# A Fourier transform and a soft mixture of experts on one core: z in token quarters with VectorE's block transposes, a in two row halves, groups of six slots, and a float32 output on 16 tiles

## The chip, the cores and the metric

The kernel runs on one core of one Trainium2 chip. The metric is device microseconds of one execution, the median over several runs. PE is TensorE (PEld its weight loads), DVE is VectorE, ACT is ScalarE, POOL is GpSimd, SP is SyncE, which issues the DMAs.

## The reference

Eight sequences of 2496 tokens with 256 values each go through a Fourier transform over the tokens and over the values, of which the real part is kept. The 19968 tokens then go through a soft mixture of eight experts with four slots each:

```
X = real(fft(fft(x, axis=1), axis=2))          # x: 8 x 2496 x 256
logits = X @ phi                               # X as 19968 x 256; 32 slots
d = exp(logits - logits.max(0)); d /= d.sum(0) + 1e-9      # over tokens
slot_input = (d.T @ X).reshape(8, 4, 256)
slot_out[e] = relu(slot_input[e] @ w1[e]) @ w2[e]          # 256 -> 1024 -> 256
c = exp(logits - logits.max(1)); c /= c.sum(1) + 1e-9      # over slots
out = c @ slot_out                             # 19968 x 256
```

All of it is in float32.

## The kernel before, in words

The transformed tokens are never formed. Since the logits are linear in x, phi is transformed first (psphi, wphi), x is multiplied with it, and the Fourier transform over the tokens is then made on 32 slot columns instead of 256 values. In the same way the weights d are transformed back and multiplied with x. The 2496 tokens are taken as 64 x 39, by a length-64 and a length-39 transform; symmetry folds 39 to 20. Two sequences are a pair (two times 64 rows), so there are four pairs, p = 0 to 3, each of five loads of x of about 1 MB into a ring of six tiles.

The program is a list of parts (ORDER), each a letter with one or two indices. A scheduler then sets the order on each engine from it.

- a(p, u) folds x on VectorE into eo (L222 to L227), transposes it on PE (pt, L231), which ScalarE copies to et (L232), and multiplies with the transformed phi on four column tiles of 32 (z, L238). ScalarE copies z to zs (L246).
- t(p) turns z back to token rows: ten PE transposes a pair (zt, L259), copied by ScalarE with a stride into the tile zt (L262, L266).
- b(p) is the length-64 transform: 11 groups of three slots of both sequences, one matmul over 128 rows each (a, L275), copied to o1 (L282).
- c(p, half) is the length-39 part: lp and lm (L293, L294), the logits lt (L295 to L298), the maxima over tokens (mx, mt, mall; L301 to L313), exp into d (L316, one a group) and its sum and difference dpm (L318, L319).
- e and d transform the weights back (e, L331, L340; d, L348) into ds (copies L356, some on VectorE); tok sums them; u multiplies with eo (L373).
- w loads w1 and w2 into the ring and the eo tiles, m merges the pairs, l and v are the experts' two layers (h, L472, with VectorE's block transpose L484; so, L492), and r replicates slot_out (sorep, L510).
- s(p) is the softmax over slots: PE turns the logits (cT, L529), ScalarE copies them to c (L534). In two halves follow the maximum (VectorE, L543), a subtraction (GpSimd, L544), exp (ScalarE, L545), the sum (VectorE, L546), 1e-9 and the reciprocal (L547, L548), and the product (GpSimd, L549).
- q(p, half) splits c into a high and a low part in a rounded float32 format, fp32r (hl, L555, L556); r did the same with slot_out (rh).
- o(p, b) is a megabyte of output: four PE transposes of hl (lT, L569), a ScalarE copy (L570), four times two matmuls of 128x512 (po, L576), eight evictions' worth of copies shared by ScalarE and VectorE (L580, 512 columns each) and the DMA (L587; the last rows of a pair go to out0, L585).

The PSUM banks of 512 columns are shared in small rings: two, three, two and one.

Of the kernel before, what the change touches and what calls it, by code (L numbers as in the profile page):

```python
# [7 lines left out]
F32R = mybir.dt.float32r  # L8
# [7 lines left out]
NPAIR = 4  # L16
D = 256
NSLOT = 32
GS = 3
NG = 11  # L20
GH = ((0, 6), (6, 5))
RING = 6
EOB = 3
CAFTER = 1
# [3 lines left out]
LT = 4  # L28
CT = ['sa', 'lt', 'lt', 'lt']
HT = ['se', 'zs']  # L30
RH = 0
LATE = 'zs'
SEB = 2
DE = 4
GP = 3
FIRST = [0, 1]
# [13 lines left out]
def _tables():  # L50
# [13 lines left out]
    eye = np.eye(2 * GS)  # L64
# [4 lines left out]
    def block(t):  # L69
# [15 lines left out]
        ("wa", np.block([[np.cos(al), np.sin(al)], [-np.sin(al), np.cos(al)]])),  # L85
# [15 lines left out]
        ("sel", np.arange(6)[:, None] + 6 * (np.arange(256) // 128) == np.tile(s, 2) // GS),  # L101
# [15 lines left out]
def _build(nc, tc, xh, phih, w1h, w2h, cins, where, out, out0):  # L117
# [4 lines left out]
    with ctx:  # L122
        cp = ctx.enter_context(tc.tile_pool(name="cp", bufs=1))
        sb = ctx.enter_context(tc.tile_pool(name="sb", bufs=1))
        pp = ctx.enter_context(tc.tile_pool(name="pp", bufs=P2, space=PSUM))
        p1 = ctx.enter_context(tc.tile_pool(name="p1", bufs=P1, space=PSUM))
        pu = ctx.enter_context(tc.tile_pool(name="pu", bufs=1, space=PSUM))
# [13 lines left out]
        def bufs_(tag):  # L141
            return {"zs": 2, "sa": 2, "se": SEB, "lt": LT}[tag]
# [7 lines left out]
        def bank1(name, dt=F32):  # L150
            return p1.tile([128, 512], dt, name=name, tag="p1")

# [45 lines left out]
        mall = cp.tile([6, 2, NPAIR, GS], F32, name="mall")  # L198
# [9 lines left out]
        zs, zt, o1, dpm, esb, dsb = {}, {}, {}, {}, {}, {}  # L208

        def part_a(p, u):  # L210
            qs = [2 * u, 2 * u + 1] if u < 2 else [4]
            nq = len(qs)
            if u == 0:
                eo[p] = [eu(f"eo{p}_{t}") for t in range(5)]
                zs[p] = sb.tile([128, 10, 128], F32, name=f"zs{p}", tag="zs", bufs=2)
            tr = []
            for k in range(2):
                tr.append(et([128, 4, 2, nq, NA], f"et{p}_{u}_{k}"))
            for qi, t in enumerate(qs):
# [8 lines left out]
                for k in range(2):  # L228
                    b = bank1(f"pt{p}_{t}_{k}")
                    for g in range(4):  # L230
                        pe.transpose(b[:, g * 128 : g * 128 + 128], e[:, g, k * 128 : k * 128 + 128], ident)  # L231
                    sc.copy(tr[k][:, :, :, qi, :], b.rearrange("p (g h a) -> p g h a", g=4, h=2))  # L232
            z = bank1(f"z{p}_{u}")
            n = 128 * nq
            for i, (w, k) in enumerate(((0, 0), (1, 1), (2, 1))):
                o = 0 if i < 2 else n
                for g in range(4):
                    pe.matmul(  # L238
                        z[32 * g : 32 * g + 32, o : o + n],
                        wphi[:, w, :],  # L240
                        tr[k][:, g].rearrange("p h q a -> p (h q a)"),
# [4 lines left out]
            sc.copy(  # L246
                zs[p][:, 4 * u * 1 : 4 * u + 2 * nq, :].rearrange("p i (r a) -> p r i a", r=2),
                z[:, : 2 * n].rearrange("p (r i a) -> p r i a", r=2, a=NA),
            )


        def part_t(p):
            zt[p] = sa([128, GS * NG, 2, NKC], f"zt{p}")
            nc.gpsimd.memset(zt[p][:, NSLOT:], 0.0)
            for b, units in enumerate(([(0, q) for q in range(4)], [(1, q) for q in range(4)], [(0, 4), (1, 4)])):
                ps = bank(f"zt{p}_{b}")
                for i, (h, q) in enumerate(units):
                    u, nq = q // 2, 2 if q < 4 else 1
                    pe.transpose(ps[:, i * 128 : i * 128 + 128], zs[p][:, 4 * u + nq * h + q % 2], ident)  # L259
                if b < 2:  # L260
                    dst = zt[p][:, :NSLOT, b, 0:16].rearrange("p s c -> p c s")
                    sc.copy(dst, ps.rearrange("p (c s) -> p c s", s=NSLOT))  # L262
                else:
                    for h in range(2):
                        dst = zt[p][:, :NSLOT, h, 16:20].rearrange("p s c -> p c s")
                        sc.copy(dst, ps[:, h * 128 : h * 128 + 128].rearrange("p (c s) -> p c s", s=NSLOT))  # L266

        def part_b(p):
            o1[p] = sa([120, 2, NG, NA], f"o1{p}")
            for b in range(3):  # L270
                ps = bank(f"a{p}_{b}")
                n = min(4, NG - 4 * b)
                for i in range(n):
                    g = 4 * b + i
                    pe.matmul(  # L275
                        ps[:120, i * 128 : i * 128 + 128],
                        zt[p][:, GS * g : GS * g + GS].rearrange("p s h c -> p (s h c)"),
                        C("wa"),
                        start=True,
                        stop=True,  # L280
                    )
                sc.copy(o1[p][:, :, 4 * b : 4 * b + n, :], ps[:120, : n * 128].rearrange("p (u r k) -> p r u k", u=n, r=2))  # L282

        def part_c(p, hf):
            g0, n = GH[hf]
            w = n * NA
            if hf == 0:
                lt[p] = sb.tile([120, NG, 2, NA], F32, name=f"lt{p}", tag="lt", bufs=LT)
            L = lt[p][:, g0 : g0 + n]
            pl = bank(f"lp{p}_{hf}")  # L290
            pm = bank(f"lm{p}_{hf}")
            mv = o1[p][:, :, g0 : g0 + n].rearrange("p r u k -> p r (u k)")
            pe.matmul(pl[:120, :w], C("wcc"), mv[:, 0], start=True, stop=True)  # L293
            pe.matmul(pm[:120, :w], C("wcs"), mv[:, 1], start=True, stop=True)  # L294
            sc.copy(L[:, :, 0], pl[:120, :w].rearrange("p (g n) -> p g n", g=n))  # L295
            pmv = pm[:120, :w].rearrange("p (g n) -> p g n", g=n)
# [3 lines left out]
            mx = sb.tile([120, 6], F32, name=f"mx{p}_{hf}", tag="mx", bufs=2)[:, :n]  # L300
            v.tensor_reduce(mx, L.rearrange("p g s n -> p g (s n)"), axis=AX.X, op=ALU.max)  # L301
            if PM:
                ps = pp.tile([128, 512], F32, name=f"mt{p}_{hf}", tag="pm", bufs=PM)
            else:
                ps = bank3(f"mt{p}_{hf}")
            pe.transpose(ps[:n, :120], mx, ident[:120, :120])
            m = mall[:n, hf, p]
            v.tensor_reduce(m, ps[:n, :120].rearrange("p (s k) -> p s k", s=GS), axis=AX.X, op=ALU.max)
            mex = sb.tile([6, GS, 40], F32, name=f"mex{p}_{hf}", tag="mex", bufs=1)[:n]
            v.tensor_scalar(mex, m.unsqueeze(2).to_broadcast([n, GS, 40]), -1.0, None, op0=ALU.mult)  # L310
            pe.transpose(ps[:120, 128 : 128 + n], mex.rearrange("p s k -> p (s k)"), ident[:n, :n])
# [3 lines left out]
            for g in range(n):  # L315
                sc.activation(d[:, g], L[:, g], AF.Exp, bias=nm[:, g : g + 1], scale=1.0)  # L316
# [341 lines left out]
```

## Time and profile before

| | us |
|---|---|
| median of 3 runs | 200.26 (199.95 to 200.35) |
| the profiled execution | 201.22 |
| its span in the profile | 199.4 |
| PE busy | 174.7 (88%) |
| VectorE, ScalarE busy | 131.8, 132.4 (66% each) |
| GpSimd busy | 24.6 (12%) |
| read from and written to HBM | 38.46 MB, 20.45 MB |

The span runs from the first to the last event that the profiler sees on the core; the profiled execution's own time holds 1.8 us more around it. The rows of the profile have the form "line engine operation out<-in shape xcount | busy, mean ns of one | idle time before, and what ended it". In a chain or a timeline a row is "start us, us, what". The mean granted clock of PE was 0.979 of full.

### The profile page before, as it was taken

The numbers are of one execution on the slowest core, as the hardware profiler recorded it, in microseconds if no ns is written. First come the engines' busy times: TensorE is split into PE (matmuls) and PEld (weight loads), VectorE is DVE, ScalarE is ACT, GpSimd is POOL, SyncE is SP. The second block draws the span as 40 slices with busy tenths as digits, with TensorE's granted clock in tenths as the row PEclk, the third lists the DMA queues.
The fourth block names the chain that finished last, engine by engine and source line by source line (L and its number), as shares of the span: only waits on it lengthen the run. The fifth ranks groups of instructions, "written<-read, shape, count | busy, mean of one in ns | idle before, by whom it ended". The sixth has DMA issues, their size and how long they took to land.

```text
span 199.4 us, 4290 instructions
## 1 busy us (share of the span) xinstructions
PE 174.7 (88%) x1690; PEld 125.6 (63%) x1690; DVE 131.8 (66%) x238; ACT 132.4 (66%) x277; POOL 24.6 (12%) x27
## 2 busy tenths in 40 slices
PE   0499889969999999989999989999999999989900
PEld 0375575549666877556865859346788877768700
DVE  0599856989993991742357624796677888976700
ACT  2135775579876795687856963763867988896610
POOL 0000000000000000000000100767101357320000
PEclk9999999997999999999999999999999999999995
DMA  5999999998880499600393687991099999799996
GB/s 183 409 427 410 422 420 420 419 391 291 301 363 21 112 358 424 263 0 0 111 283 138 205 326 234 364 404 58 2 378 355 419 409 389 306 421 363 430 426 214
DMA packets 10707, 59.17 MB, mean 297 GB/s; under 512 B 1344, under 2 KB 1728, under 8 KB 5696
## 3 DMA queue, kind: packets, MB, share of 16 engines
q1 hardware_dynamic: 10688, 58.91, 76.0%
q8 instruction: 13, 0.21, 0.4%
q14 instruction: 6, 0.05, 0.1%
HBM read 38.46 MB, written 20.45 MB: 295 GB/s over the span
## 4 chain that ended last, share of the span: by engine, by line
PE 75%; ACT 10%; DMA 2%; DVE 2%; issue 2%; POOL 2%; SPq 0%; ACTq 0%; DVEq 0%; POOLq 0%
PE po L576 17%; PE pt L231 9%; PE z L238 7%; PE a L275 6%; PE e L331 6%; PE u L373 5%; PE d L348 4%; PE h L472 4%; PE so L492 3%; PE lp L293 3%; PE lm L294 3%; PE cT L529 2%; DMA x<-xh 2%; ACT zt L262 2%; PE lT L569 2%
## 5 line engine op out<-in xcount | busy, mean ns | idle before, releaser
L576 PE MATMUL po<-rh,lTs 128*128 128x512 f32 x160 | 42.4, 405 | 1.5 <-ACT lTs L570 0.7
L231 PE MATMUL pt<-cs,eo 128*128 128x128 f32 x160 | 26.9, 300 | 8.9 <-DVE eo L226 7.9
L576 PEld LDWEIGHTS po<-rh,lTs 128*128 128x128 f32 x160 | 28.1, 188 | 8.5 <-ACT o L580 1.8
L232 ACT COPY et<-pt 128x512 f32<-128x512 f32 x40 | 23.1, 592 | 13.8 <-PE pt L231 13.2
L580 DVE COPY o<-po 128x512 f32<-128x512 f32 (+1 forms) x40 | 26.9, 686 | 7.9 <-PE po L576 7.0
L231 PEld LDWEIGHTS pt<-cs,eo 128*128 128x128 f32 x160 | 19.9, 153 | 15.9 <-DVE eo L226 7.9
L580 ACT COPY o<-po 128x512 f32<-128x512 f32 x40 | 23.2, 595 | 7.3 <-PE po L576 7.1
L224 DVE TENSOR_TENSOR x<-x 128x1024 f32<-128x1024 f32 x16 | 19.5, 1217 | 3.0 <-DMA x<-xh 3.0
L238 PE MATMUL z<-et,wphi 128*32 128x256 f32 (+1 forms) x288 | 19.0, 371 | 1.9 <-ACT et L232 1.8
L544 POOL TENSOR_TENSOR c<-c,cm 128x640 f32<-128x640 f32 x8 | 11.8, 1489 | 28.0 <-DVE cm L543 27.0
L316 ACT ACTIVATE d<-lt,nm 120x128 f32<-120x128 f32 x44 | 13.6, 390 | 1.9 <-DVE nm L313 1.8
L226 DVE TENSOR_TENSOR eo<-x 128x512 f32<-128x512 f32 x20 | 13.6, 682 | 0.6 <-PE u L373 0.3
L238 PEld LDWEIGHTS z<-et,wphi 128*32 128x32 f32 x288 | 7.8, 113 | 9.4 <-ACT et L232 4.2
L227 DVE TENSOR_TENSOR eo<-x 128x512 f32<-128x512 f32 x20 | 13.6, 680 | 0.0
L331 PE MATMUL e<-cs,dpm 120*64 120x120 f32 x176 | 13.5, 273 | 0.0
L331 PEld LDWEIGHTS e<-cs,dpm 120*64 120x64 f32 x176 | 10.7, 136 | 3.5 <-issue 2.4
L356 ACT COPY ds<-d 64x320 f32<-64x320 f32 x24 | 10.0, 421 | 4.2 <-PE d L348 3.5
L275 PE MATMUL a<-cs,zt 128*120 128x128 f32 x88 | 12.2, 292 | 0.4 <-ACT zt L266 0.3
L275 PEld LDWEIGHTS a<-cs,zt 128*120 128x120 f32 x88 | 11.1, 196 | 1.9 <-ACT zt L266 1.3
L549 POOL TENSOR_TENSOR c<-c,cm 128x640 f32<-128x640 f32 x8 | 11.0, 1391 | 10.0 <-DVE cm L548 5.5
L570 ACT CAST lTs<-lT 128x512 fp32r<-128x512 f32 x20 | 11.5, 599 | 0.9 <-PE lT L569 0.9
L373 PE MATMUL u<-eo,ds 128*32 128x129 f32 x320 | 11.6, 275 | 0.0
(99 smaller groups left out, 251.4 us busy)
## 6 DMA issues: line engine op xcount, KB each, us to landing
x<-xh SPq DMA_DIRECT2D x16, 1024.0 KB, 11.3
out<-o SPq DMA_DIRECT2D x15, 1024.0 KB, 5.6
w<-w1h SPq DMA_DIRECT2D x6, 1024.0 KB, 8.6
w<-w2h SPq DMA_DIRECT2D x12, 512.0 KB, 6.0
x<-xh SPq DMA_DIRECT2D x4, 896.0 KB, 10.3
out<-o SPq DMA_DIRECT2D x4, 768.0 KB, 6.0
w<-w1h SPq DMA_DIRECT2D x4, 512.0 KB, 5.2
w<-w2h SPq DMA_DIRECT2D x2, 1024.0 KB, 8.0
```

The costliest lines, as they stand in the source:

```text
L224: v.tensor_tensor(x[:, 0:4], x[:, 0:4], x[:, 4:8], op=ALU.add)
L226: v.tensor_tensor(e[:, :, 0:128], x[:, 0:4, 0:128], x[:, 0:4, 128:256], op=ALU.add)
L227: v.tensor_tensor(e[:, :, 128:256], x[:, 0:4, 0:128], x[:, 0:4, 128:256], op=ALU.subtract)
L231: pe.transpose(b[:, g * 128 : g * 128 + 128], e[:, g, k * 128 : k * 128 + 128], ident)
L232: sc.copy(tr[k][:, :, :, qi, :], b.rearrange("p (g h a) -> p g h a", g=4, h=2))
L238: pe.matmul(z[32 * g : 32 * g + 32, o : o + n], wphi[:, w, :], tr[k][:, g].rearrange("p h q a -> p (h q a)"), start=i != 1, stop=i != 0, t ...
L275: pe.matmul(ps[:120, i * 128 : i * 128 + 128], zt[p][:, GS * g : GS * g + GS].rearrange("p s h c -> p (s h c)"), C("wa"), start=True, stop ...
L316: sc.activation(d[:, g], L[:, g], AF.Exp, bias=nm[:, g : g + 1], scale=1.0)
L331: pe.matmul(ps[64 * k : 64 * k + 64, 120 * i : 120 * i + 120], dpm[p, hf][:, k, 3 * j + i, :], C(name), start=True, stop=True, tile_positi ...
L373: last = pe.matmul(ub[32 * g : 32 * g + 32, 0:129], dsb[p][:, k, c, :], e[:, 0:129] if k == 0 else e[:, 127:256], start=cc == 0, stop=cc == 9,
L576: pe.matmul(po, lT[:, i, :], rh[j].rearrange("p k d -> p (k d)"), start=j == 0, stop=j == 1,)
L580: (v.tensor_copy if n_ev[0] % 2 else sc.copy)(ot[:np_, 2 * i : 2 * i + 2, :].rearrange("p k d -> p (k d)"), po[:np_])
```

## The change

Four things change together.

Part t is gone. In a, the moving side of z takes 32 tokens of each of the eight (or four) row groups (a token quarter) on each column tile, so that VectorE's transposes of 32x32 blocks bring z straight from PSUM to zt, two transposes a part (24 in all: 16 of 128x256 and 8 of 128x128). zs and its copies go as well.

Groups have six slots of one sequence instead of three slots of two: six groups a sequence, with the last padded. In b, each of the two sequences has its own 64 rows of PE, and the real and imaginary part are added up in PSUM (96 matmuls in place of 44). A float32 matmul is two instructions in the trace, so these are 192 and 88. exp works on 24 tiles of 120x256 in place of 44 of 120x128. e has 192 instructions in place of 176. lp and lm are 384 columns wide throughout. d is made in two column halves of PE, with 16 ScalarE copies of 128x320 in place of 24 on ScalarE and 8 on VectorE of 64x320.

The output takes c and slot_out in plain float32. q is a VectorE block transpose (128x640), and o makes 32 matmuls a megabyte, each 32 rows by 32 columns of PE with 256 moving columns, on all 16 tiles over a piece. The PSUM rings are closed after r and four tiles of two banks take their place. Evictions are of 1024 columns, the first half on ScalarE, the second on VectorE (both on ScalarE for b = 3). The first piece is sent in two DMAs of 512 KB. The tokens of each output row are other ones, which the host undoes.

In ORDER, s20 moves from after o10 to before o02, s30 from after o14 to before o11, and q is held back to after an output piece of the pair before.

```diff
-    "o04 o10 s20 q11 o11 q20 o12 o13 q21 o14 s30 o20 o21 q30 o22 o23 "
+    "u30 m00 l00 s00 l10 q00 s10 v00 v10 r00 o00 q01 o01 q10 s20 o02 "
+    "q11 o03 o04 o10 s30 o11 q20 o12 q21 o13 o14 o20 o21 q30 o22 q31 "
...
-                        tr[k][:, g].rearrange("p h q a -> p (h q a)"),
+                        tr[k][:, :, 32 * g : 32 * g + 32],
...
-            sc.copy(
-                zs[p][:, 4 * u * 1 : 4 * u + 2 * nq, :].rearrange("p i (r a) -> p r i a", r=2),
...
+            for r in range(2):
+                v.transpose(zt[p][:, r, :NSLOT, 8 * u : 8 * u + n].rearrange("p s c -> p c s"), z[:, r])
...
+                    for h in range(2):
+                        rows = slice(64 * h, 64 * h + 64)
+                        pe.matmul(
+                            ps[h][:120, : 2 * HG * NA].rearrange("p (r g k) -> p g r k", r=2, g=HG)[:, g],
+                            zt[p][rows, r, s0 : s0 + GS].rearrange("p s c -> p (s c)"),
+                            wa[rows, 128 * r : 128 * r + 128],
+                            start=r == 0,
+                            stop=r == 1,
+                            tile_position=(64 * h, 0),
+                        )
...
         def part_o(p, b):
+            for i, ev in ((0, sc.copy), (1, sc.copy if b == 3 else v.tensor_copy)):
+                src = two(f"po{p}_{b}_{i}")
+                for gi in range(2):
+                    for j in range(4):
+                        for u in range(2):
+                            q = 2 * i + u
+                            r = slice(32 * q, 32 * q + 32)
+                            pe.matmul(
+                                src[32 * j : 32 * j + 32, u, 256 * gi : 256 * gi + 256],
+                                tl[p][r, 8 * b + 4 * gi + j, :], rep[r, :],
+                                start=True, stop=True, tile_position=(32 * q, 32 * j),
+                            )
```

In the changed kernel the z matmuls stand at L238, the transposes into zt at L247, a at L259, exp at L297, cT at L511, the maximum, sum and reciprocal at L524, L527 and L529, GpSimd's two steps at L525 and L530, the transpose of c at L537, po at L553, the evictions at L559 and L563.

How instructions stand on VectorE at the start of the output, before (o0_2 is the tile of output piece p = 0, b = 2; cm2_0 holds the maxima and sums of the first half of pair 2):

```order
L580 COPY o0_1_1722<-po0_1_3_1735 128x512
L580 COPY o0_2_1750<-po0_2_1_1755 128x512
L580 COPY o0_2_1750<-po0_2_3_1763 128x512
L580 COPY o0_3_1775<-po0_3_1_1780 128x512
L580 COPY o0_3_1775<-po0_3_3_1788 128x512
L580 COPY o0_4_1800<-po0_4_1_1805 128x512
L580 COPY o0_4_1800<-po0_4_3_1814 64x512
L543 TENSOR_REDUCE cm2_0_1862<-c2_1844 128x20
L543 TENSOR_REDUCE cm2_1_1870<-c2_1844 128x20
```

And after, at the same place:

```order
L559 COPY o0_0_1681<-po0_0_1_1701 128x1024
L559 COPY o0_1_1721<-po0_1_1_1740 128x1024
L537 STREAM_TRANSPOSE tl1_1759<-c1_1565 128x640
L524 TENSOR_REDUCE cm2_0_1780<-c2_1761 128x20
L524 TENSOR_REDUCE cm2_1_1788<-c2_1761 128x20
L527 TENSOR_REDUCE cm2_0_1780<-c2_1761 128x20
L559 COPY o0_2_1796<-po0_2_1_1815 128x1024
```

The maxima of pair 2 and the first of its sums have moved from behind all evictions of pair 0 to ahead of that of o0_2.

On PE at the first b of the program, before (zt and pt are PE transposes, a the length-64 transform):

```order
L259 MATMUL zt0_2_284<-cs0_70,zs0_146 128x128 x2
L231 MATMUL pt1_0_1_306<-cs0_70,eo1_0_289 128x128 x4
L275 MATMUL a0_0_342<-cs2_72,zt0_270 120x128 x4
L275 MATMUL a0_1_348<-cs2_72,zt0_270 120x128 x4
L275 MATMUL a0_2_354<-cs2_72,zt0_270 120x128 x3
```

And after (a0_0_1 is half 0 of the groups, sequence 1):

```order
L259 MATMUL a0_0_0_328<-cs2_72,zt0_145 120x2x64
L259 MATMUL a0_0_1_329<-cs2_72,zt0_145 120x2x64
L259 MATMUL a0_1_0_345<-cs2_72,zt0_145 120x2x64 x6
L231 MATMUL pt1_1_0_300<-cs0_70,eo1_1_274 128x128 x4
L259 MATMUL a0_1_1_346<-cs2_72,zt0_145 120x2x64 x5
```

The two sequences alternate for the first half of the groups (the first two rows come six times over), and in the second half one sequence comes after the other, with transposes between.

More of the change, by code (lines that the diff above doesn't have):

```diff
@@ new lines, in part_b @@
+        def part_b(p, hf):
+            o1[p, hf] = sb.tile([120, 2, 2, HG * NA], F32, name=f"o1{p}_{hf}", tag="o1", bufs=O1)
+            ps = [bank(f"a{p}_{hf}_{h}") for h in range(2)]
+            wa = C("wa")
+            for g in range(HG):
+                s0 = GS * (HG * hf + g)
+                for r in range(2):
+                    for h in range(2):
+                        rows = slice(64 * h, 64 * h + 64)
[8 more added lines that the diff above has]
+            for h in range(2):
+                sc.copy(o1[p, hf][:, h].rearrange("p r n -> p (r n)"), ps[h][:120, : 2 * HG * NA])
@@ L293, in part_c @@
[L293 to L296, printed above, removed]
+            pe.matmul(pl[:120, :n], C("wcc"), o1[p, hf][:, :, 0], start=True, stop=True)
+            pe.matmul(pm[:120, :n], C("wcs"), o1[p, hf][:, :, 1], start=True, stop=True)
+            sc.copy(L[:, :, 0], pl[:120, :n].rearrange("p (g n) -> p g n", n=NA))
@@ new lines, in part_c @@
+            pe.transpose(ps[:120, 128 : 128 + HG], mex.rearrange("p s k -> p (s k)"), ident[:HG, :HG])
+            nm = sb.tile([120, HG], F32, name=f"nm{p}_{hf}", tag="nm", bufs=2)
+            v.tensor_copy(nm, ps[:120, 128 : 128 + HG])
+            d = sb.tile([120, 2, HG, 2, NA], F32, name=f"d{p}_{hf}", tag="d", bufs=2)
+            for g in range(HG):
+                sc.activation(
+                    d[:, :, g].rearrange("p h s n -> p h (s n)"),
+                    lt[p][:, hf, :, g].rearrange("p h s n -> p h (s n)"),
+                    AF.Exp, bias=nm[:, g : g + 1], scale=1.0,
+                )
@@ L598, in after @@
+                        ot[:, k0:k1],
+                    )
+            if b == 4:
+                nc.sync.dma_start(out0[p].rearrange("p (r d) -> p r d", d=D), ot[:64, 6:8])
+        def after(what, f, *a):
+            with tc.issue_after(anchor[what]):
                 return f(*a)
         parts = {
-            "a": part_a, "t": lambda p, _: part_t(p), "b": lambda p, _: part_b(p), "c": part_c,
+            "a": part_a, "b": part_b, "c": part_c,
             "e": part_e, "d": part_d, "u": lambda p, _: part_u(p), "w": lambda *_: load_w(),
@@ L644 @@
     r = _run(nc, [arrays], core_ids=[0])
-    got = r.results[0]["out"].reshape(NPAIR, 2, NA, 19, 2, D)
-    got0 = r.results[0]["out0"].reshape(NPAIR, NA, 2, D)
+    rows = r.results[0]["out"].reshape(NPAIR, 4, 32, 38, D).transpose(0, 3, 2, 1, 4)
+    rest = r.results[0]["out0"].reshape(NPAIR, 2, 32, 2, D).transpose(0, 3, 2, 1, 4)
+    place = np.zeros((NPAIR, 4, 32, 10, 4, D), np.float32)
+    for q in range(4):
+        for g in range(9):
+            row = 8 * (g // 2) + 2 * q + g % 2 if g < 8 else (32, 34, 36, 37)[q]
+            place[:, q, :, g] = rows[:, row]
+        if q < 2:
+            place[:, q, :, 9] = rows[:, 33 + 2 * q]
+        else:
+            place[:, q, :, 9, :2] = rest[:, q - 2]
+    place = place.reshape(NPAIR, 2, NA, NKC, 2, D)
+    got, got0 = place[:, :, :, :19], place[:, 0, :, 19]
     full = np.empty((NPAIR, 2, 2496, D), np.float32)
```

280 lines of the change are left out of this document (107 added, 173 removed), and 9 rows, old and new, of the table ORDER.

## The prediction

> **What bounds the kernel now.** I read the page first (busy shares, the chain that ended last), then the windows by stage, then the list of waits, and last the chain and the timelines at the places that the change touches. The page says that TensorE (PE) carries the chain:
>
> ```profile
> PE 174.7 (88%) x1690; PEld 125.6 (63%) x1690; DVE 131.8 (66%) x238; ACT 132.4 (66%) x277; POOL 24.6 (12%) x27
> PE 75%; ACT 10%; DMA 2%; DVE 2%; issue 2%; POOL 2%; SPq 0%; ACTq 0%; DVEq 0%; POOLq 0%
> ```
>
> A mean over the span hides stages. The windows split it (columns: busy time of PE, weight loads, VectorE, ScalarE, GpSimd, then granted clock, DMA share, GB/s):
>
> ```profile
> 10.00:60.00 50.00, 46.17 (x420) 32.18 (x423) 44.07 (x67) 33.76 (x68) 0.26 (x2) 0.97 0.97 385
> 60.00:122.00 62.00, 60.01 (x781) 43.19 (x774) 33.25 (x77) 44.46 (x112) 1.20 (x3) 1.00 0.51 184
> 144.00:199.40 55.40, 44.57 (x238) 34.93 (x236) 35.66 (x60) 37.67 (x70) 11.16 (x8) 0.95 0.92 370
> 144.00:146.00 2.00, 2.00 (x13) 1.64 (x12) 1.76 (x4) 1.63 (x3) 0.00 (x0) 1.00 0.62 236
> 184.00:188.00 4.00, 4.00 (x22) 3.37 (x21) 3.33 (x5) 2.35 (x5) 0.00 (x0) 1.00 1.02 428
> 196.00:199.40 3.40, 0.00 (x0) 0.00 (x0) 0.00 (x0) 0.00 (x0) 0.00 (x0) 0.50 0.48 198
> ```
>
> Three stages, three limits. Until 60 the loads fill the queues (0.97) and VectorE is busy 44.1 of 50. From 60 to 122 PE is busy 60.0 of 62. From 144 the output's DMA is busy 0.92: 51.0 of 55.4 us, idle 4.4, of which 0.8 (144 to 146, at 0.62) and 1.8 (196 on, at 0.48) lie at its ends and 1.8 inside. At the full rate of the 184:188 row, 428 GB/s, the 20.45 MB of output need 47.8 us, so the end can't come more than 3.2 us of DMA work sooner than now, whatever PE does there.
>
> So two questions decide: what the change does to PE and VectorE before the last expert matmul, and whether it keeps the output's DMA fed. The last matmul of so ends at 139.5, and the first output matmul starts at 141.86:
>
> ```profile
> 133.65 5.84 PE so L492 x109
> 141.86 2.53 PE po L576 x10
> ```
>
> **Part by part: PE in the front.** Durations from the chain (start, length, count):
>
> ```profile
> 17.77 0.44 PE zt L259 x4
> 26.46 2.73 PE a L275 x22
> 53.00 1.43 PE e L331 x24
> 69.22 0.54 PE lp L293 x2
> 79.39 0.65 PE lm L294 x2
> 71.17 0.88 PE a L275 x8
> ```
>
> The 40 zt transposes go: 40 x 0.11 = -4.4 us. The a matmuls were 88 instructions at 0.11 (0.88 / 8). They become 192 over 64 rows each. If the two row halves run beside each other they fill 96 places, 10.6 us against 9.7, +0.9. The order puts the second group's halves one after the other, so those may not pair: 48 + 96 places, 15.8 us, +6.1. No row of this trace shows row halves; I take the middle, +3.5. e grows by 16 instructions of 0.06, +1.0. Four halves of lp and lm go from 320 to 384 columns: 4 x 2 x 0.11 = +0.9. cT has 12 transposes a pair for 11: 4 x 0.11 = +0.4. z, d and u keep their columns. PE's own sum is +1.4 (-1.2 to +4.0).
>
> **ScalarE leaves the chain.** What PE waited for up to 122:
>
> ```profile
> PE z L238 <- ACT et L232: 1.8, 2, 1.6
> PE zt L259 <- ACT zs L246: 1.4, 2, 1.0
> PE pt L231 <- ACT zs L246: 0.7, 1, 0.7
> PE tok L363 <- ACT ds L356: 0.7, 1, 0.7
> PE a L275 <- ACT zt L266: 0.3, 1, 0.3
> ```
>
> The zs and zt rows are 2.4 us; the 1.8 stood behind a zt copy of 2.16 us on ScalarE. The copies disappear, but z's result now waits in VectorE's row behind the folds, so the a stage can wait there. I credit 1.9 of the 4.2. Front on PE: +1.4 - 1.9 = -0.5 us. The d and exp edits shorten ScalarE, which only pays through these same waits.
>
> **VectorE in the front.** It gains 24 block transposes. The operation itself is in the trace, from SBUF to SBUF and contiguous; the folds give the scale with size:
>
> ```profile
> L484 DVE STREAM_TRANSPOSE hT<-hs 128x512 f32<-128x512 f32 x4 | 2.7, 678 | 0.1
> L224 DVE TENSOR_TENSOR x<-x 128x1024 f32<-128x1024 f32 x16 | 19.5, 1217 | 3.0 <-DMA x<-xh 3.0
> L226 DVE TENSOR_TENSOR eo<-x 128x512 f32<-128x512 f32 x20 | 13.6, 682 | 0.6 <-PE u L373 0.3
> 22.65 1.23 DVE L224 TENSOR_TENSOR x<-x 128x1024 f32<-128x1024 f32 x1 [0.86 <-DMA x<-xh]
> 26.42 1.22 DVE L224 TENSOR_TENSOR x<-x 128x1024 f32<-128x1024 f32 x1 [1.22 <-DMA x<-xh]
> 31.47 0.55 DVE L297 TENSOR_TENSOR lt<-lt,lm 120x384 f32<-120x384 f32 x1 [2.49 <-PE lm L294]
> 62.22 0.48 DVE L356 COPY ds<-d 64x320 f32<-64x320 f32 x1 [2.37 <-PE d L348]
> 63.29 0.48 DVE L356 COPY ds<-d 64x320 f32<-64x320 f32 x1 [0.59 <-PE d L348]
> ```
>
> 512 elements more cost 0.535 us, so an estimate is 0.41 for 128x256 and 0.28 for 128x128. Before the last fold (about 73) stand the transposes of three pairs: 12 x 0.41 + 6 x 0.28 = 6.6 us, less the two ds copies above, 1.0. The idle time in the rows above is 7.5 us. So 5.6 us would fit, and I count 0; without that cover it costs up to +5.6. A transpose that writes with stride could cost more (the third rival).
>
> **The output stage.** PE first. A 256-column matmul instruction on one of four column tiles took 5.84 / 109 = 54 ns. A megabyte piece of output now has 64 such instructions: 3.43 us with four tiles at once, 1.71 with eight. I take 1.71, since each half of a piece uses two row quarters. DMA needs 2.45 us a megabyte, so PE stays hidden. Evictions of 1024 columns cost two of the old ones, about 1.2 us, one on each engine: hidden too. The lT copies and the hi/lo split go, off the path.
>
> What is not hidden is VectorE's row. Before, ten evictions of tokens of pair 0 stood ahead of the maxima for pair 2. Now both maxima and the first sum of pair 2 stand ahead of the eviction of o0_2, and that sum waits for ScalarE, which waits for GpSimd. The same chain, once in the trace with VectorE free, and GpSimd's step once with VectorE busy:
>
> ```profile
> 123.82 1.54 DVE L543 TENSOR_REDUCE cm<-c 128x20 f32<-128x640 f32 x2 [0.52 <-ACT c L534]
> 124.72 2.49 POOL L544 TENSOR_TENSOR c<-c,cm 128x640 f32<-128x640 f32 x2 [9.90 <-DVE cm L543]
> 126.02 0.74 ACT L545 ACTIVATE c<-c 128x640 f32<-128x640 f32 x1
> 126.79 0.82 DVE L546 TENSOR_REDUCE cm<-c 128x20 f32<-128x640 f32 x1 [1.33 <-ACT c L545]
> 165.96 3.67 POOL L544 TENSOR_TENSOR c<-c,cm 128x640 f32<-128x640 f32 x2 [2.62 <-DVE cm L543]
> ```
>
> From the last copy of c to the end of the sum: 127.6 - 123.8 = 3.8 us, or 0.6 more with the slower GpSimd step. With E for the end of so: the first po at E+2.4, o0_0 and o0_1 take PE to E+5.8, twelve cT transposes to E+7.1, the four copies of c on ScalarE (360 or 280 columns, at about 0.4: an estimate from the 0.59 for 512 columns in the L232 row below), behind o0_1's first eviction, to E+8.5. Then 3.8 to the sum's end and 1.2 for the eviction: the DMA of o0_2 is issued at E+13.5 and flows about 1.1 later, as the first did. Until then two megabytes are queued, flowing from about E+5.3: they run out at E+10.2. The queue is dry for 4.0 to 4.4 us. Pair 3's chain before o1_1 repeats it with more pieces queued, 1.3 to 2.0, and tl2, which waits for GpSimd's product, before o1_2: 0.8 to 1.0. In all 6.1 to 7.4; I take 6.4, near the chain with VectorE idle. DMA busy is between 47.8 and 51.0, say 49.4. The stage: 49.4 + 2.6 (ends) + 6.4 = 58.4 us, against 55.4: +3.0.
>
> **The sum.** Span 199.4 - 0.5 + 3.0 = 201.9. The profiled execution took 201.22 us, 1.8 above its span; the median of the runs is 200.26, 0.9 above that span. So 201.9 + 0.9 = 202.8 us.
>
> **Rivals.** *First, faster: ScalarE's relief is worth all of it.* The waits of PE above (4.9 us) all go, the row halves of a pair up throughout (PE's sum is then -1.2), VectorE's idle time takes the transposes: up to 6.1 off the front, 5.0 if a wait or two stays, and the output loses 2.5. Span 199.4 - 5.0 + 2.5 = 196.9, time 197.8. For it: ScalarE was the second engine of the chain (10%). Against: VectorE inherits the work in the stage in which it is the busiest. It decides if a starts no later than now after the last z.
>
> *Second, much slower: row tiles don't run side by side.* Then a piece takes 3.43 us on PE, more than its 2.45 of DMA: 20 x 3.43 = 68.6 us from E+2.4, and the end near 217. Against it: column tiles do overlap here (54 ns is a quarter of 0.21). No row of before has row tiles. The Trainium skill, "TensorE: Matmul & The Clock Gate", Part 3 (Packing small matmuls), reports 3.07 times for four row tiles and 10.6 times for sixteen tiles, so this rival gets little.
>
> *Third, slower: the transposes write z's slots with a stride of one token row and cost double.* On ScalarE a strided copy did:
>
> ```profile
> L262 ACT COPY zt<-zt 128x512 f32<-128x512 f32 x8 | 8.7, 1202 | 0.6 <-PE zt L259 0.6
> L232 ACT COPY et<-pt 128x512 f32<-128x512 f32 x40 | 23.1, 592 | 13.8 <-PE pt L231 13.2
> ```
>
> That adds 6.6 us to VectorE before the last fold, where 7.5 - 5.6 = 1.9 of idle would be left: +4.7, 207.5. It decides once the folds come later than the loads.
>
> *Fourth, slower: PE's clock drops in the dry stretches.* With four PSUM tiles filled, PE waits about 5 us for the eviction of o0_2. The 196:199.4 row has the clock at 0.50 with PE idle. If it halves at each of the three waits, a piece takes 3.43 us instead of 2.45 of DMA, one or two pieces: about +2, 204.8. The Trainium skill, "TensorE: Matmul & The Clock Gate", Part 1, puts the drop after an idle window of about 3.4 us; the idle end of this trace agrees.
>
> **How the numbers follow.** Forecast 0.44, first rival 0.33, second 0.05, third 0.11, fourth 0.07. About 0.2% (0.4 us) is what a measurement here can tell from no change; between 199.9 and 200.7 fall the edges of the forecast (0.04) and of the first rival (0.03), 0.07. Another 0.04 of the forecast lies below that. Faster 0.30 + 0.04 = 0.34, slower 0.40 - 0.04 + 0.05 + 0.11 + 0.07 = 0.59. The range runs from 196.5, the first rival with all 6.1 off the front, to 208.0, just above the third; the second rival and the tails, under 2 in 10, stay outside. Signs differ within it, so the forecast's own range: 200.5 to 205.0.
>
> **What would show it.** Right: so ends between 138 and 140; a dip of DMA to near zero for about 4 us some ten us after so ends, while VectorE idles before the sum of pair 2 and the eviction of o0_2 follows it; a smaller dip at o1_1; a piece's po matmuls near 1.7 us; z transposes near 0.4 us. Wrong: so ends before 137 (first rival), the DMA stays at 0.9 through o0_2, po near 3.4 us (second), transposes near 0.8 us (third), clock well below 1 between 150 and 190 (fourth).

## The result, and the profile after

The changed kernel takes 217.48 us (216.45 to 218.41, four runs) against 200.31 in the same job: a ratio of 1.0846, 95% interval 1.0776 to 1.0917. It is slower by 17 us where 2.5 were forecast, and lies outside the range. Executions of one kernel with the float32 output spread by up to 3%; those over 1.5% above the fastest count as slow, and the ratios are of the others, medians and ranges of all. The profiled execution took 216.45 us, with a span of 214.7. Its page, three lines:

```profile
PE 173.9 (81%) x2846; PEld 116.0 (54%) x2846; DVE 131.2 (61%) x228; ACT 98.2 (46%) x184; POOL 21.1 (10%) x25
q8 instruction: 22, 0.36, 0.7%
PE 68%; DVE 14%; issue 6%; ACT 5%; DMA 2%; POOL 1%; SPq 0%; DVEq 0%; ACTq 0%
```

ScalarE's work went down as meant, 132.4 to 98.2 us. PE's busy time is the same with 1156 more matmul instructions. Two things are new on the chain: VectorE with 14% and "issue", time in which an engine waits for nothing that the profile shows, with 6% (2% each before). The queue of instruction blocks carried 22 packets of 16 KB; before it was 13, on a line of the page that the prediction didn't use:

```profile
q8 instruction: 13, 0.21, 0.4%
```

The chain of the changed kernel, where so ends and po begins, and two stretches of a (start, length, count):

```profile
102.05 1.28 PE a L259 x18
106.78 2.48 PE a L259 x24
140.88 6.09 PE so L474 x112
149.01 3.06 PE po L553 x111
```

so ends at 147.0 against 139.5: the front has lost 7.5 us. From there to the end of the span it is 67.7 us against 59.9: the output has lost 7.8. The two make the 15.3 us between the spans.

**The front.** The groups of a and of the transposes (matmuls of PE, busy us, mean ns, then idle before), after:

```profile
L259 PE MATMUL a<-cs,zt 64*120 64x128 f32 x192 | 19.7, 282 | 1.8 <-ACT o L268 1.5 <-DVE zt L247 0.3
L247 DVE STREAM_TRANSPOSE zt<-z 128x256 f32<-128x256 f32 x16 | 9.9, 705 | 7.6 <-PE z L238 7.6
L247 DVE STREAM_TRANSPOSE zt<-z 128x128 f32<-128x128 f32 x8 | 2.8, 437 | 1.4 <-PE z L238 1.4
```

and of the same work before:

```profile
L275 PE MATMUL a<-cs,zt 128*120 128x128 f32 x88 | 12.2, 292 | 0.4 <-ACT zt L266 0.3
L259 PE MATMUL zt<-cs,zs 128*128 128x128 f32 x40 | 7.2, 284 | 1.4 <-ACT zs L246 1.4
```

a grew by 7.5 us of busy time; the zt transposes gave back 7.2. In the chain 24 instructions of a took 2.48 us, 103 ns each, and 18 others 1.28, 71 ns: some run beside each other, most don't. What PE waits for up to 129, the wait for the first folds (8.3 us; 7.9 before) left aside:

```profile
PE pt L231 <- ACT et L232: 2.9, 4, 0.7
PE e L315 <- DVE dpm L304: 1.8, 1, 1.8
PE a L259 <- ACT o L268: 1.5, 2, 0.9
PE z L238 <- ACT et L232: 1.0, 2, 0.6
PE lm L278 <- ACT lt L279: 0.6, 1, 0.6
```

These are 7.8 us; the rows of before were 4.9. The groups above overlap where one operation follows another, so the whole front is better read from PE's busy time up to the end of so, before and after:

```profile
0.00:139.53 139.53, 125.82 (x1427) 87.19 (x1428) 93.67 (x174) 90.83 (x199) 12.54 (x19) 0.99 0.73 277
0.00:146.97 146.97, 129.94 (x1540) 87.11 (x1540) 99.78 (x188) 68.04 (x146) 10.06 (x17) 1.00 0.69 264
```

PE is busy for 4.1 us more and idle for 3.3 us more (17.0 against 13.7). The two are the front's loss.

**The output.** VectorE where the forecast saw the stall (start, length), and the windows of it, of the later one and of the whole stage (columns as in the prediction):

```profile
155.14 1.55 DVE L524 TENSOR_REDUCE cm<-c 128x20 f32<-128x640 f32 x2 [1.06 <-ACT c L517]
158.11 0.82 DVE L527 TENSOR_REDUCE cm<-c 128x20 f32<-128x640 f32 x1 [1.42 <-ACT c L526]
158.84 1.22 DVE L559 COPY o<-po 128x1024 f32<-128x1024 f32 x1
```

```profile
151.00:214.70 63.70, 41.28 (x1225) 26.89 (x1205) 30.73 (x38) 28.88 (x36) 9.94 (x8) 0.77 0.82 324
157.70:161.00 3.30, 0.89 (x41) 0.75 (x49) 2.89 (x5) 2.82 (x5) 0.83 (x1) 1.00 0.08 30
171.40:174.30 2.90, 2.17 (x91) 1.33 (x66) 2.90 (x5) 2.44 (x3) 0.42 (x1) 0.91 0.11 45
```

The DMA is dry (0.08, 0.11) for 3.3 us behind the sum of pair 2 and for 2.9 behind that of pair 3. PE's clock over the stage is 0.77. And further on PE stands still with every operand there (idle time and its cause in brackets):

```profile
176.54 4.45 PE L553 MATMUL po<-rep,tl 32*32 32x256 f32 x205 [1.34 <-DVE o L559]
185.15 4.43 PE L553 MATMUL po<-rep,tl 32*32 32x256 f32 x128 [4.16 <-issue]
192.44 4.57 PE L553 MATMUL po<-rep,tl 32*32 32x256 f32 x128 [2.86 <-issue]
197.54 3.07 PE L553 MATMUL po<-rep,tl 32*32 32x256 f32 x128 [0.53 <-issue]
202.36 3.75 PE L553 MATMUL po<-rep,tl 32*32 32x256 f32 x83 [1.75 <-issue]
```

Read the counts: between two waits stand 128 matmuls each time. With as many weight loads these are 256 instructions, and in 16 KB that makes 64 bytes an instruction: one block of the instruction queue. In the trace the blocks' packets start at 182.8, 190.0, 195.3 and 199.9, and PE goes on 2.3 to 2.5 us after each. PE waits for its own program. A block feeds two megabytes of output, which the DMA drains in 4.9 us; here blocks begin to run 7.3, 5.1 and 4.8 us apart. The time of a block's own matmuls lies inside that: the packets at 195.3 and 199.9 start before PE has finished the block before.

Whether such a wait costs the kernel anything is read from the DMA. The first row holds the waits of 4.16 and 2.86 us, the second comes right behind them:

```profile
177.40:195.30 17.90, 10.88 (x383) 7.63 (x367) 7.26 (x7) 6.21 (x7) 0.30 (x1) 0.82 1.00 401
195.30:196.60 1.30, 1.30 (x66) 0.95 (x52) 0.62 (x2) 0.78 (x1) 0.00 (x0) 0.79 0.22 90
```

Pieces that were finished earlier were still queued, so the DMA stayed full through both waits and ran dry only once, for 1.0 us. By the packets of the trace the DMA is dry for 7.2 us between the output's first and last flow: 6.2 in three stretches behind VectorE's sums and the rest of pair 3's chain (from 157.7, 171.4 and 176.9), and 1.0 behind the code (from 195.3). Before it was 1.2. So of the 7.8 us that the output lost, some 6.0 are dry time; the DMA's busy time is 1.2 longer (52.4 against 51.2), and the rest lies at the ends.

### The profile page after: what moved, and what is told of

Its sections match the earlier page's. It is cut to its first block, busy times and chain, and to the rows that moved or that the text cites. A ratio compares the mean times of both kernels' runs of the same rounds, so it can differ in the third digit from the quotient of the medians.

```text
span 214.7 us, 6450 instructions
## 1 busy us (share of the span) xinstructions
PE 173.9 (81%) x2846; PEld 116.0 (54%) x2846; DVE 131.2 (61%) x228; ACT 98.2 (46%) x184; POOL 21.1 (10%) x25
## 4 chain that ended last, share of the span: by engine, by line
PE 68%; DVE 14%; issue 6%; ACT 5%; DMA 2%; POOL 1%; SPq 0%; DVEq 0%; ACTq 0%
PE po L553 14%; PE pt L231 8%; PE a L259 7%; PE z L238 6%; PE e L315 6%; PE d L334 5%; PE u L357 4%; PE h L454 3%; PE cT L511 3%; PE so L474 3%; PE lp L277 3%; DMA x<-xh 2%; DVE eo L226 2%; PE lm L278 2%; DVE o L559 2%
## 5 line engine op out<-in xcount | busy, mean ns | idle before, releaser
L553 PE MATMUL po<-rep,tl 32*32 32x256 f32 x1280 | 39.2, 458 | 14.5 <-issue 9.3
L553 PEld LDWEIGHTS po<-rep,tl 32*32 32x32 f32 x1280 | 25.2, 116 | 26.3 <-issue 14.2
L231 PE MATMUL pt<-cs,eo 128*128 128x128 f32 x160 | 26.0, 297 | 11.2 <-DVE eo L226 8.3
L559 ACT COPY o<-po 128x1024 f32<-128x1024 f32 x24 | 23.7, 1012 | 20.3 <-PE po L553 20.1
L259 PE MATMUL a<-cs,zt 64*120 64x128 f32 x192 | 19.7, 282 | 1.8 <-ACT o L268 1.5
L559 DVE COPY o<-po 128x1024 f32<-128x1024 f32 x12 | 14.6, 1217 | 8.3 <-PE po L553 8.1
L238 PE MATMUL z<-et,wphi 128*32 128x256 f32 (+1 forms) x288 | 18.4, 360 | 1.2 <-ACT et L232 1.0
L525 POOL TENSOR_TENSOR c<-c,cm 128x640 f32<-128x640 f32 x8 | 10.0, 1264 | 93.7 <-DVE cm L524 93.7
L259 PEld LDWEIGHTS a<-cs,zt 64*120 64x120 f32 x192 | 16.6, 179 | 4.8 <-ACT o L268 2.5
L247 DVE STREAM_TRANSPOSE zt<-z 128x256 f32<-128x256 f32 (+1 forms) x24 | 12.7, 616 | 9.0 <-PE z L238 9.0
L226 DVE TENSOR_TENSOR eo<-x 128x512 f32<-128x512 f32 x20 | 13.7, 683 | 0.3
L297 ACT ACTIVATE d<-lt,nm 120x256 f32<-120x256 f32 x24 | 10.5, 498 | 5.4 <-DVE nm L294 5.3
L238 PEld LDWEIGHTS z<-et,wphi 128*32 128x32 f32 x288 | 7.6, 111 | 9.4 <-ACT et L232 4.2
L334 PE MATMUL d<-e,cs 128*64 128x320 f32 x64 | 11.9, 444 | 0.0
L563 DVE COPY o<-po 128x1024 f32<-128x1024 f32 x4 | 4.8, 1208 | 11.4 <-issue 5.8
## 6 DMA issues: line engine op xcount, KB each, us to landing
x<-xh SPq DMA_DIRECT2D x4, 896.0 KB, 11.3
```

The source lines that it names most:

```text
L226: v.tensor_tensor(e[:, :, 0:128], x[:, 0:4, 0:128], x[:, 0:4, 128:256], op=ALU.add)
L238: pe.matmul(z[32 * g : 32 * g + 32, i // 2], wphi[:, w, :], tr[k][:, :, 32 * g : 32 * g + 32], start=i != 1, stop=i != 0, tile_position=(0 ...
L259: pe.matmul(ps[h][:120, : 2 * HG * NA].rearrange("p (r g k) -> p g r k", r=2, g=HG)[:, g], zt[p][rows, r, s0 : s0 + GS].rearrange("p s c - ...
L334: pe.matmul(ps[64 * h : 64 * h + 64, :320], C("wb")[:, 64 * k : 64 * k + 64], esb[p][:, h].rearrange("p g n -> p (g n)")[:, 320 * hf : 320 ...
L553: pe.matmul(src[32 * j : 32 * j + 32, u, 256 * gi : 256 * gi + 256], tl[p][r, 8 * b + 4 * gi + j, :], rep[r, :], start=True, stop=True, ti ...
L559: done = ev(ot[:, 4 * i : 4 * i + 4].rearrange("p k d -> p (k d)"), src.rearrange("p q n -> p (q n)"))
```

## The experiments

Where a median and a profile are compared below, the profile's own stages are used. "Stage" is the time from the end of so to the end of the span: 59.9 before, 67.7 after.

**The order put back** (s20 to after o10, s30 to after o14):

```diff
-    "... v10 r00 o00 q01 o01 q10 s20 o02 q11 o03 o04 o10 s30 o11 q20 o12 q21 o13 o14 o20 ..."
+    "... v10 r00 o00 q01 o01 q10 o02 q11 o03 o04 o10 s20 o11 q20 o12 q21 o13 o14 s30 o20 ..."
```

> The changed kernel, with the softmax of pairs 2 and 3 back at the places in the order that they had before (after o10 and o14). Theory A (VectorE's row: the sum of pair 2 ahead of the eviction of o0_2, that of pair 3 ahead of o1_1, starve the output's DMA for 3.35 + 2.95 us): both dry stretches shrink to about 1 us in all, and the time falls by 4 to 6 us, to 211.5 to 213.5. Theory B (TensorE's instruction blocks of 16 KB arrive late behind the output's own packets, and what isn't lost in the dry stretches is lost waiting for code): the dry stretches shrink, but TensorE's waits that the profile calls issue grow from 9.3 us, and the time falls by less than 2.5 us, to 215 or more.

Measured: 219.3 us (215.9 to 222.2), no clear gain; stage 70.8 in the profiled execution, which took 222.2. PE's timeline where o0_2 had stood behind the sum, and near the end:

```profile
162.69 2.19 PE L553 MATMUL po<-rep,tl 32*32 32x256 f32 x59 [3.13 <-issue]
207.66 3.49 PE L553 MATMUL po<-rep,tl 32*32 32x256 f32 x83 [4.22 <-issue]
```

The stall at o0_2 is gone, and PE waits 3.13 us for code there; the DMA is busy at 0.99 in that wait (159.6 to 162.7). But the stall itself has only moved. VectorE later, and the DMA in the two stretches where pair 2's and pair 3's sums stand:

```profile
170.01 1.55 DVE L524 TENSOR_REDUCE cm<-c 128x20 f32<-128x640 f32 x2 [3.86 <-ACT c L517]
172.98 0.82 DVE L527 TENSOR_REDUCE cm<-c 128x20 f32<-128x640 f32 x1 [1.42 <-ACT c L526]
173.71 1.21 DVE L559 COPY o<-po 128x1024 f32<-128x1024 f32 x1
```

```profile
170.40:175.90 5.50, 5.01 (x165) 3.34 (x154) 4.08 (x8) 4.22 (x5) 2.49 (x2) 0.66 0.09 34
187.70:192.40 4.70, 3.05 (x145) 2.20 (x129) 3.21 (x7) 3.52 (x5) 2.21 (x2) 1.00 0.06 21
```

Counting the evictions, the sum of pair 2 now stands ahead of that of o1_1, and that of pair 3 ahead of that of o2_0. The DMA is dry for 11.3 us in all, against 7.2 in the changed kernel, where theory A had about 1 us. So the edit didn't take away what theory A blames, and the run says nothing against it. Theory B's waits didn't grow either (9.2 us; 9.3 before). The wait for code and the half clock from 164 to 174 delay the copies that VectorE's maxima wait for; how much of the dry time is theirs isn't shown.

**a's halves in turn.** Each matmul of a is held back to after the one before it in the source, so that the halves alternate throughout:

```diff
+            last = None
...
-                        pe.matmul(
+                      with tc.issue_after(last.ins) if last is not None else nullcontext():
+                        last = pe.matmul(
```

> The changed kernel, with the two row halves of a forced to alternate, one matmul of each. Theory A (the front is longer because most halves stand one after the other and run one at a time, 109 ns each, instead of two in 109 ns): the a matmuls take some 11 us instead of 18.6, the last matmul of so ends near 140 instead of 147.0, and the time falls by 5 to 7.5 us, to 210 to 212.5. Rival (the front waits for VectorE's transposes and ScalarE's evictions, and TensorE's time is only filled differently): so ends less than 2 us earlier and the time falls by less than 2 us.

Measured: 214.87 us (212.4 to 215.7), ratio 1.0656 (1.0566 to 1.0746); so ends at 145.5.

```profile
L261 PE MATMUL a<-cs,zt 64*120 64x128 f32 x192 | 15.6, 283 | 2.0 <-ACT o L270 1.7 <-DVE zt L247 0.3
```

a's busy time falls by 4.1 us, to 15.6, not to 11. In the trace the two halves of a pair now start 7 ns apart, and pairs follow at 109 ns; but the first of each run and the last before another operation take 200 ns, and a is cut into many runs. That lies between the two expectations: the pairing counts, and its size was put too high. The front is 1.5 us shorter: PE's busy time up to the end of so falls by 2.1, and its idle time grows by 0.6. The clock in this execution was 0.91 from 110 to 130 (1.00 in the changed kernel's); that it took the rest is likely, not shown.

**Both edits.**

> Both edits of the two kernels before. If the losses in the front and in the output are separate, their gains add up: by theory A 9 to 13 us, 204.5 to 208.5. If code loading bounds the output, the gain is about that of the paired halves alone plus at most 2.5: 207.5 to 211.

Measured: 216.74 us (213.8 to 219.5), ratio 1.0691 (1.0593 to 1.0789): no better than the paired kernel alone (214.87), so the gains don't add up; of the two expected ranges, 204.5 to 208.5 and 207.5 to 211, neither holds. The waits called issue are 8.9 us, but the order put back brings its own loss here too: the DMA is dry for 11.2 us in the same two places, against 8.1 in the kernel with a's halves in turn alone. The run doesn't decide between the stall and the code.

**Half the output's instructions**: order put back, and c and slot_out rounded to bfloat16 for the output matmuls, which takes one pass instead of two.

```diff
-            rep = sb.tile([128, D], F32, name="rep", tag="d", bufs=2)
+            rep = sb.tile([128, D], BF, name="rep", tag="d", bufs=2)
...
-                nc.gpsimd.tensor_tensor(c, c, m[:, 1].unsqueeze(2).to_broadcast([128, 20, NSLOT]), op=ALU.mult)
+                    cr[p][:, 20 * i : 20 * i + 20], c, m[:, 1].unsqueeze(2).to_broadcast([128, 20, NSLOT]), op=ALU.mult
```

> The first kernel (order put back), with c and slot_out rounded to bfloat16 for the output matmuls: one pass instead of two, so half of the output's TensorE instructions, 640 matmuls with as many weight loads, about five blocks of code less; the output is rounded to that format. Theory B (code loading): the waits called issue fall from several us to under 2, and the time is 2 to 6 us below the first kernel's. Rival (the granted clock, which was 0.69 to 0.79 from 165 on): TensorE is still less busy here, the clock is as low or lower, and the time is within 1 us of the first kernel's.

Measured: 208.77 us (207.5 to 209.9), ratio 1.0392 (1.0324 to 1.046). so ends at 148.5, the stage is 58.1 us.

```profile
153.00:206.60 53.60, 21.26 (x576) 10.05 (x567) 28.36 (x37) 26.87 (x34) 9.94 (x8) 0.50 0.95 382
```

That is 10.5 us below the order put back in float32, where 2 to 6 were expected. The list of waits has no row "issue" for po any more. The clock is 0.50 in all of the stage, lower than in the changed kernel, and the DMA is busy 0.95 and never dry from its first flow to its last. So a low clock alone doesn't make the output long; with half of the passes PE has time to spare, though, and what the clock costs the float32 output isn't shown. Nor is it shown that the fewer instructions helped, for VectorE's row is another one here. Two evictions, of o1_1 and o1_2 by count, stand ahead of pair 2's sums:

```profile
162.68 2.34 DVE L564 COPY o<-po 128x1024 f32<-128x1024 f32 x2
164.94 1.53 DVE L528 TENSOR_REDUCE cm<-c 128x20 f32<-128x640 f32 x2
```

Code waits and stalls both went; the next run brings the first back.

**As many instructions again, with few columns**: the kernel before, each output matmul cut in two.

```diff
-                            pe.matmul(
-                                src[32 * j : 32 * j + 32, u, 256 * gi : 256 * gi + 256],
+                            for y in range(2):
+                                pe.matmul(
+                                    src[32 * j : 32 * j + 32, u, 256 * gi + 128 * y : 256 * gi + 128 * y + 128],
```

> The bfloat16 kernel before (208.8 us), with each output matmul cut into two of 128 columns: as many output instructions as in float32 (1280 matmuls with as many weight loads), but TensorE's columns of the bfloat16 kernel, half of the float32 one's or less. The output is rounded as there. If the code decides (theory B), the time goes back up to 213 to 219 and the waits called issue come back, several us of them. If TensorE's time for the columns at a low clock decided, the time stays within 2 us of 208.8.

Measured: 211.85 us (209.6 to 212.3), ratio 1.0551 (1.0486 to 1.0615); stage 60.5.

```profile
PE po L559 <- issue: 16.6, 7, 4.4
```

The waits for code are back, longer than ever, but the time rises by 3 us only, short of the 213 expected. With little to do per block (1.9 to 2.4 us for 128 matmuls in the trace), PE spends on waiting what it spent on columns. The DMA hardly notices:

```profile
154.10:207.50 53.40, 26.43 (x1135) 19.07 (x1112) 29.14 (x37) 26.79 (x34) 10.04 (x8) 0.50 0.97 384
```

It is busy at 0.99 in the longest wait (189.2 to 193.6) and dry once, for 1.4 us. So 16.6 us of waits for code lengthen the stage by 2.4 us. By this run they are not what made the float32 output 8 us longer.

**Twice the instructions in float32**, by the same cut.

> The first kernel (order put back, float32), with each output matmul cut into two of 128 columns: twice the output's instructions, 20 blocks of 16 KB instead of 10, for about the same TensorE columns. Theory B: each megabyte now needs a whole block, and the output stage gets much longer, by 20 to 50 us (time 235 to 270). Rival (columns and clock): within 5 us of the first kernel's 219.

Measured: 255.64 us, one run; stage 104.7.

```profile
160.00:170.00 10.00, 9.40 (x290) 8.82 (x291) 1.98 (x2) 3.04 (x3) 0.00 (x0) 0.50 0.56 225
```

As theory B had it in size, but not by code: PE is busy 9.4 of 10 us here and makes 290 matmuls of 128 columns, about 34 ns each at a clock of 0.50; the waits for code are 8.5 us of the whole stage. In the changed kernel 91 matmuls of 256 columns start in the 3.4 us of low clock from 192.4 on, some 37 ns each. So half the columns didn't make a matmul half as long, and twice as many take nearly twice as long. Here PE's own time bounds the output.

**Few writes**: order put back, float32, with one of eight rows of each piece sent; the rest of the output isn't written.

```diff
+                    k1 = k0 + 1
                     nc.sync.dma_start(
```

> The first kernel (order put back, float32), that leaves out seven eighths of the output's transfers (one of eight rows of each piece is sent; the rest of the output isn't written). If blocks of code come late because they stand behind the output's packets, the waits called issue fall from 9.2 us to under 1.5 and the last output matmul comes within 45 us of the end of so (before 61). If a block takes its time whatever the DMA does, these waits stay above 5 us, since TensorE has nothing else to wait for.

Measured: 204.05 us, one run. The last po comes 50.7 us after so, not within 45, since PE waits for VectorE here:

```profile
PE po L553 <- DVE o L559: 6.2, 5, 2.5
PE po L553 <- issue: 1.9, 3, 0.9
```

The waits for code are 1.9 us instead of 9.2, just above the bound that was set: with the queues nearly empty a block comes almost in time. The packets show it too. Where a wait marks the start of a block (153.6, 157.3, 195.4), the packet of the next one starts 1.1 to 1.2 us later; in the changed kernel (185.2, 192.4, 197.5, 202.4) it is 2.4 to 4.8. That the output's own packets delay the blocks is shown by that, in one execution of each; how (the share of the queues, the order of packets) is not.

**Front of before, output in bfloat16.**

> The front of the kernel before (part t, groups of three slots, a over 128 rows) with the output of the bfloat16 kernel (order put back; the output is rounded to bfloat16 factors). If front and output are separate terms: so ends at 139 to 140 as before, the output stage takes the 58.5 us that it took in the bfloat16 kernel, and the time is 198 to 200.5, at or just below the kernel before. If the longer front of the changed kernel came from the output's part of the code (its order, its buffers), so ends later than 143 here as well, and the time is above 203.

Measured, twelve runs: 198.97 us (197.9 to 199.8) against 200.46, ratio 0.9937 (0.9911 to 0.9962): below before by 0.6%, clear of the spread.

```profile
134.29 5.88 PE so L497 x109
```

so ends at 140.2, the stage is 57.8. Front and output are separate terms. The DMA is never dry here from 145 to 195, and this output is 2 us shorter than the old one; but its factors are rounded to bfloat16.

**a's halves in turn, with the bfloat16 output.**

> The bfloat16 kernel (order put back; 208.8 us, 1.039 of before), with the row halves of a forced to alternate as in the second kernel. Its output waits for no code, so the front shows undisturbed. Theory A': the unpaired halves cost 4 us of TensorE's time, of which the second kernel gave some back by a lower clock at the end of the front: the time falls by 2.5 to 4.5 us, to 204.5 to 206.5. Rival (the front's length is set by the waits at its end, for exp and its sums): less than 1.5 us.

Measured: 205.32 us (205.0 to 205.7), ratio 1.0253 (1.0207 to 1.0299), 3.4 below 208.77: theory A' holds for the time. so ends at 146.5 against 148.5, which is the 2 us that the pairing is worth in the front; the stage is 0.9 shorter.

**The sums first, with the bfloat16 output**: VectorE's evictions of o0_2 and o1_1 are held back to after the sums of pairs 2 and 3.

```diff
+                    first = {(0, 2, 1): "sum20", (1, 1, 1): "sum30"}.get((p, b, i))
+                    with tc.issue_after(anchor[first]) if first else nullcontext():
```

> The bfloat16 output in the order of the changed kernel, with the evictions of the second half of o0_2 and o1_1 on VectorE forced to stand behind the sums of pairs 2 and 3, as they do in the changed kernel. The output is rounded to bfloat16 factors. If the prediction's term was sized right, the output's DMA runs dry for about 3.3 and 2.9 us there and the time is 4 to 6 us above the bfloat16 kernel's 208.8. If these waits were dear only beside the late code, the time is within 2 us of 208.8.

Measured: 210.15 us (208.5 to 212.3), ratio 1.041 (1.0342 to 1.0477): 1.4 us above by the medians, where 4 to 6 were expected. In the profiled execution (211.8 us) the DMA is dry once, at o0_2, and the stage is 61.2 where it was 58.1:

```profile
158.70:161.60 2.90, 0.64 (x19) 0.15 (x16) 1.81 (x2) 2.58 (x4) 1.51 (x2) 0.50 0.09 37
```

At o1_1 other evictions had come ahead, so that the second stall didn't form. In this one execution a stall of 2.9 us lengthens the stage by about as much; two of the four took 208.47 us, no more than without it, so the price isn't clear of the spread.

**Front of before, float32 output of the changed kernel.**

> The front of the kernel before with the float32 output of the changed kernel, in its order (an extra tile for the product of the softmax aside). If front and output are separate terms, so ends at 139 to 140, the output stage takes 66 to 70 us as in the changed kernel, with several us of waits for code, and the time is 207 to 211, 7 us below the changed kernel. If the two are coupled (the clock or the code position carried over from the front), the output stage differs by over 4 us from 68.

Measured: 209.53 us (206.0 to 210.2), ratio 1.0362 (1.0253 to 1.047). so ends at 139.6, the stage is 68.8 us: as in the changed kernel, with 4.6 us of waits for code, and the DMA dry for 8.4. The two losses add up: 9.6 us here for the output, and 8.0 more in the changed kernel for the front.

**The profiled executions side by side**, without those of twice the instructions and of few writes (us; dry is the DMA's idle time in stretches between the output's first and last flow, from the packets of each trace):

| kernel | time | stage | DMA dry | PE waits for code |
|---|---|---|---|---|
| before | 201.2 | 59.9 | 1.2 | none |
| changed | 216.5 | 67.7 | 7.2 | 9.3 |
| order put back | 222.2 | 70.8 | 11.3 | 9.2 |
| a's halves in turn | 215.7 | 68.4 | 8.1 | 6.5 |
| both edits | 217.8 | 70.4 | 11.2 | 8.9 |
| bfloat16 output | 208.5 | 58.1 | 0 | none |
| bfloat16, matmuls cut in two | 211.8 | 60.5 | 1.4 | 16.6 |
| bfloat16, a's halves in turn | 205.5 | 57.2 | 0 | none |
| bfloat16, sums first | 211.8 | 61.2 | 2.8 | none |
| front of before, bfloat16 | 199.8 | 57.8 | 0 | none |
| front of before, float32 | 210.2 | 68.8 | 8.4 | 4.6 |

The stage less the dry time is 57.2 to 60.5 us in every row, while the waits for code go from none to 16.6. The output's length follows the DMA's dry stretches. No run has the float32 output with the evictions ahead of the sums, so whether the late code would then show is open.

## Why the prediction was wrong, point by point

*What bounds each stage* was read rightly, and so was the question that decides. The forecast of 202.8 missed by 14.7 us: the front by 8.0 (-0.5 forecast, +7.5 measured), the output by 4.8 (+3.0 and +7.8), and the step from the span to the median by 1.9 (0.9 before, where the profiled execution stood above every run, 2.8 after, where it was the lowest).

*PE in the front* was put at +1.4; its busy time up to the end of so rose by 4.1. a was taken at +3.5, the middle of two bounds; its group cost +7.5 of busy time, above the upper bound of 6.1. The order that was quoted shows the halves one after the other, and that was the row to go by: 109 ns unpaired. Missing was that each change between a and another operation costs 200 ns instead of 109. Alternating them brings back 4.1 us of a's busy time, of which 2 reach the end of so in the bfloat16 kernels. The group of the transposes gave 7.2 us back, not 4.4: they were counted by their own 110 ns, without the same changes. d was put at nothing, since it keeps its columns; it has 64 instructions instead of 32, and its group grew from 10.4 to 11.9 us.

*ScalarE's relief* was credited with 1.9 us. This is the step that failed most: PE's idle time up to the end of so rose by 3.3 us, 5.2 from the forecast and in the other direction. The waits for zs and zt went, and others came: 7.8 us against 4.9. PE now waits for ScalarE's copies of pt (2.9), for the evictions of a (1.5), which are four of 384 columns where there were three, and at the end of the front for exp and its sum (1.8). The prediction took ScalarE's shorter work for shorter waits. What each of the new waits costs is read from the trace and tested by no run.

*VectorE in the front* had the transposes at 0.41 and 0.28 us; they took 0.705 and 0.437, part of the way to the third rival. It was busy 47.3 us from 10 to 60 (44.1 before), and PE's waits for the transposes themselves are 0.3 (in the row of a): the cover was there.

*The output's stall* came where it was put and in its size: dry for 3.3 and 2.9 us at o0_2 and o1_1 and 0.5 at o1_2, 6.7 in all against 6.4. What was mis-sized are the terms beside it. The DMA's busy time was taken at 49.4 us, the middle between the full rate and the 51.0 of before, though nothing in the change makes the transfers faster; measured were 52.2 (0.82 of 63.7). Beside the stall no idle time was left inside the stage; another 1.0 came behind the code. These two make 3.8 of the 4.8 us; the rest lies at the ends of the stage.

*"PE stays hidden"* was right for the matmuls at full clock: the timeline has 128 in 3.06 us from 149.01 on, which is 23.9 ns each and 1.53 us a piece, where 1.71 was forecast. It left out that a piece has 64 matmuls and 64 weight loads to be fetched. The page of before had the queue of instructions with 13 packets. PE waited 9.3 us for code, but the DMA was full in these waits except for 1.0 us.

*The rivals.* The second rival's 217 is the measured time by luck, and its mechanism is refuted: 23.9 ns is less than half of 54, so eight tiles run at once. The fourth had the clock right (0.79 from 165 to 190); its price in float32 isn't shown. A block of 128 took 4.43 us with the clock at 0.50 for 3.4 of them (from 185.15) and 3.07 at the full clock (from 197.54), but in the bfloat16 kernels the clock is at 0.50 through the whole output and the stage is the shortest. The Trainium skill, "Runtime: NRT & Kernel Launch", section "Instruction fetch mechanics", says that the instruction memory is refilled in 16 KB blocks of 256 instructions, which the trace agrees with (128 matmuls and 128 weight loads between waits), and that crossing a block is mostly hidden. For PE it isn't here, with 9.3 us of waits; for the output's DMA it nearly is.

*Open:* what each of the front's new waits costs, whether late code would lengthen the float32 output once the sums don't, and why the clock is low with 32x32 tiles while PE's row is nearly full.

## What to carry to other kernels

A wait costs something only where it reaches the engine that ends last. Here PE's waits for code were long and new, and the easiest to blame, while the DMA that bounds the output was full in them; so read the DMA's share in the very window of a wait before calling it the cause. When an edit is meant to remove a stall, look in its trace whether the stall is gone or has moved. Less work on an engine isn't fewer waits for it: give a credit only where a row shows what would come next. Cutting a matmul into small tiles multiplies instructions: count them, and look on the page how many instruction packets there are. Tiles that can run beside each other do so only where they stand next to each other in the order, so read the pairing off the order before taking it into a sum.

## What was not expected of the hardware

A block of 256 PE instructions was followed by waits of up to 4.2 us with the output's DMA full, and of at most 0.9 with few writes. Two matmuls over 64 rows each start 7 ns apart, and one pair follows the other at 109 ns; eight with 32x32 tiles start 7 to 11 ns apart as well. A change between a and PE's transposes costs about 200 ns. With 32x32 tiles the granted clock went to 0.50 with PE busy 9.4 of 10 us, where before it was 1.00 with PE busy 60.0 of 62 and larger tiles. A float32 matmul on such a tile took about 34 ns with 128 columns and 37 with 256 at that clock. A block transpose from PSUM with strided writes took 705 ns for 128x256, where one of 128x512 in SBUF took 678.
